# An attention and gated-convolution kernel: loads on ScalarE spaced by the transfer in front of them, and a new order of the work

## The chip, the cores and the metric

The kernel runs on one core of a Trainium2 chip. The time is that of the device in microseconds, from three runs; beside it stands one execution that the hardware profiler recorded.

## The reference, cut to what matters

```python
B, N, m, C = 4, 12800, 32, 128                 # x is B x N x C, I is m x C
def mab(q, kv):                                # attention, scale = 1 / sqrt(C)
    a = softmax(scale * q @ kv.T)              # over the last axis, less its maximum
    return a @ kv
h = mab(I, x)                                  # 32 rows for each of the 4 batches
x1 = mab(x, h)
gate = sigmoid(sum(conv_w[k] * shift(x1, 4 - k) for k in range(5)))   # along N, causal
out = (gate * (x1 @ w_val)) @ w_out
```

## The kernel before

The 12800 positions of a batch are cut into four strips of 3200, and each strip into seven or eight chunks of 128 to 480 positions; the four strips of a chunk are worked on together. Chunk c of batch b is written (b, c). Each chunk is loaded twice: transposed (`xt`, 0.70 to 0.98 MB, line 392), for the scores, and with positions on the partitions (`xk`, line 404), for the weighted sums; most chunks of batch 0 have their `xk` made on TensorE from `xt` instead (L431).

The work has items, which the list `ORDER` puts in a row: `s1` (scores of the 32 inducing rows against a chunk, L456), `gm` (their maximum), `h` (weighted sum over a chunk, L523), `u`, `w`, `W`, `po` (small steps once a batch: normalise h, fold w_val, the taps and w_out into weights), `s2` (scores of a chunk against h, L718, and a softmax over 32 on VectorE, GpSimd and ScalarE, up to the fp16 halves P1 and P2, L791 and L798), `r` (a block of gate matmuls, L812, for one chunk, with the value matmuls, L821, of the chunk before), `o` (the output projection of one strip of a chunk, L922 to L924, and its eviction from PSUM, L937 on VectorE or L939 on ScalarE), `x` and `k` (make or load an `xk`), `z` (idle matmuls on zeros, L976) and `raw` (load of the weights). An `l` item loads a chunk if it isn't loaded yet; all of them stand behind the first use of their chunk, so they do nothing.

`ORDER` fixes TensorE's order. The orders of the other engines come from a planner, `Plan.lay`, at build time: it plays all operations through with costs, gives each engine the ready one that is due first (less a bias from `URGE`), and the program is emitted in that order. Nothing of the planner runs on the chip. In it `bus` is the time at which the transfers issued so far are through, and `line` the same for stores. A load is an operation of SyncE before the first `r` item and of ScalarE after it, a store (L957) of SyncE, apart from two at the end. Engines work in their own order, so an operation that waits holds up what is behind it on that engine. The list `OUTV` says which evictions go to VectorE.

The number of buffers bounds how far an engine runs ahead: 11 for `xt`, 4 for `xk`, 6 for the evicted output (`os`), 4 PSUM banks (`a`) for scores, values and outputs. An eviction waits until the store of the tile six before it has landed; the PSUM bank that it reads stays taken so long.

Of the kernel before, what the change touches and what calls it, by code (L numbers as in the profile page):

```python
# [40 lines left out]
PAGE, PAGE_AT, PAGE_TIME = 256, 20, 1.0  # L41
LAND, LAND_OUT = 3.2, 2.0
# [9 lines left out]
class Plan:  # L52
# [15 lines left out]
    def op(self, eng, dur, fn, deps=(), early=0.0, new=(), use=(), lag=None, kind=None, behind=(), steps=0, dma=None):  # L68
# [71 lines left out]
    def lay(self, deps, succ, topo, nominal):  # L140
# [18 lines left out]
        free, bus, steps = dict.fromkeys(("PE", "DVE", "ACT", "POOL"), 0.75), 1.45, -PAGE_AT  # L159
# [10 lines left out]
        while len(seq) < n:  # L170
            best = None
            for e, lst in pools.items():
                if not lst:
                    continue
                start = max(free.get(e, 0.0), min(r for r, _ in lst))
                if e == "PE":
                    w = len(wants[lst[0][1]])
# [56 lines left out]
def tile_kernel(ctx: ExitStack, tc: tile.TileContext, xt, xk, indT_in, w64, out):  # L234
# [211 lines left out]
    def s1(b, c, bank="a"):  # L446
# [21 lines left out]
    def gmax(b, g):  # L468
# [18 lines left out]
        i = PE(16, 0.17, f1, [i, i_const], [key], [m1], "strips", 0.2)  # L487
# [51 lines left out]
    def prep(b):  # L539
# [32 lines left out]
        i = PE(8, 0.42, f3, [i, i_const], [key], [Hs[-1]], lag=0.2)  # L572
# [9 lines left out]
    def prep2(b):  # L582
# [7 lines left out]
        i4 = PE(4, 0.28, f4, [ix["hT", b], iw], [key], [("hT", b)], lag=0.15)  # L590
# [46 lines left out]
    def prep3(b, e):  # L637
# [8 lines left out]
        i6 = PE(48, 0.35, f6, ix[w2][e], [key], [w2], lag=0.25)  # L646
# [13 lines left out]
    def prep_out(b):  # L660
# [13 lines left out]
        i = PE(16, 0.24, f1, [i, i_mask], [key], [dq], "strips", 0.2)  # L674
# [151 lines left out]
    def rblock(k, *starts):  # L826
# [11 lines left out]
        for lo, hi in zip(cuts, cuts[1:]):  # L838
# [20 lines left out]
            i = PE(2 * len(todo), max(spent), f, list(dict.fromkeys(deps)), new, use, "rows", 0.34)  # L859
# [43 lines left out]
    def outp(k, r):  # L903
# [9 lines left out]
        if last:  # L913
# [3 lines left out]
            i = PE(4, 1.06 / 512 * n, f, [ix["gv", b, c, r], ix["wo", b]], [key], [tg, ("wof", b)])  # L917
        else:
# [7 lines left out]
            i = PE(6, COST["out"] * n, f, [ix[g2], ix["wo", b]], [key], [g1, g2, ("wo", b)])  # L926
# [4 lines left out]
        def ev():  # L931
            if new:
# [34 lines left out]
    PE(2 * WARM, 0.43 * WARM, warm_up, [i_zero], [("a", "warm")])  # L967

    def idle(k, n):
# [8 lines left out]
        PE(2 * n, 0.216 * n, f, [], [key])  # L978
# [202 lines left out]
```

## Time and profile before

| | |
|---|---|
| median of 3 runs | 289.60 us (289.21 to 289.81) |
| the profiled execution | 289.35 us, of which the span from the first to the last instruction is 287.6 us |
| granted clock of TensorE, mean over the span | 0.988 |
| TensorE busy | 273.8 us (95%) |
| VectorE busy | 231.4 us (80%) |
| GpSimd busy | 207.9 us (72%) |
| ScalarE busy | 197.7 us (69%) |
| moved by DMA | 75.41 MB (48.56 read, 26.21 written by the instructions' account) |

Matmuls are pipelined, and the profile models their ends, so "busy" on TensorE says that it has matmuls under way. The granted clock is 1.00 at 2.4 GHz and 0.50 at 1.2 GHz. Time of an engine that is not on the chain which ended last costs nothing by itself.

### The profile page before, as it was taken

Reading aid. Unit: us, or ns where it says so; the run is one execution under the profiler, and the core shown is the slowest. Engines: PE = TensorE matmul, PEld = TensorE weight load, DVE = VectorE, ACT = ScalarE, POOL = GpSimd, SP = SyncE. Lnnn points to the kernel's source line nnn. Section 1 sums busy time; section 2 is a strip of 40 time slices with the busy share of each in tenths; the row PEclk is TensorE's granted clock in tenths of the full one; section 3 lists DMA queues with packets and bytes.
Section 4 is the critical chain, followed back from the end, with each engine's and each line's share of the span. In section 5 each row is a group of like instructions: output and inputs, shape, how many; then the busy total and the mean of one; then the engine's idle time right before and its main releaser. Section 6 shows DMA issues by size and latency. Waiting matters only on the chain.

```text
span 287.6 us, 10037 instructions
## 1 busy us (share of the span) xinstructions
PE 273.8 (95%) x4123; PEld 143.0 (50%) x4123; DVE 231.4 (80%) x541; ACT 197.7 (69%) x299; POOL 207.9 (72%) x236
## 2 busy tenths in 40 slices
PE   8989798999998999999699999999999999999998
PEld 2658345555544555575234645474444444444543
DVE  1558789989888999879389999879878999876861
ACT  2547159577657887877519886996876987777662
POOL 2000467998686799976736998988898999989650
PEclk9999889999999999999979999999999999999999
DMA  7999998988997788899955988604252224434437
GB/s 289 424 416 417 413 421 318 345 316 276 397 370 265 220 285 315 266 388 411 389 202 167 336 305 294 249 9 171 96 200 92 98 98 171 168 134 174 173 137 273
DMA packets 24493, 75.41 MB, mean 262 GB/s; under 512 B 2816, under 2 KB 17664, under 8 KB 24448
## 3 DMA queue, kind: packets, MB, share of 16 engines
q1 hardware_dynamic: 19120, 42.03, 37.9%
q10 hardware_dynamic: 5328, 32.75, 31.4%
q8 instruction: 32, 0.52, 0.7%
q14 instruction: 13, 0.11, 0.1%
HBM read 48.56 MB, written 26.21 MB: 260 GB/s over the span
## 4 chain that ended last, share of the span: by engine, by line
PE 76%; DVE 10%; DMA 9%; issue 2%; ACT 1%; POOL 1%; ACTq 0%; DVEq 0%; POOLq 0%
PE g L812 22%; DMA out_dram<-os 9%; PE a L523 8%; PE a L718 7%; PE a L456 7%; PE a L922 7%; PE a L924 6%; PE a L923 6%; PE a L821 4%; PE g L431 3%; DVE tg L881 2%; PE g L976 2%; DVE os L937 1%; PE a L965 1%; DVE ss L464 1%
## 5 line engine op out<-in xcount | busy, mean ns | idle before, releaser
L899 POOL TENSOR_TENSOR gl<-tg,gh 128x960 f16<-128x960 f32 (+4 forms) x56 | 104.7, 1882 | 14.0 <-PE a L924 7.8
L812 PE MATMUL g<-P,W 32*128 32x480 f16 (+4 forms) x1740 | 103.4, 345 | 1.0 <-POOL P L798 0.7
L881 DVE SCALAR_TENSOR_TENSOR tg<-tg,a 128x480 f32<-128x480 f32 (+4 forms) x116 | 65.5, 601 | 10.1 <-PE a L821 8.9
L812 PEld LDWEIGHTS <-W 32*128 32x128 f16 x1740 | 51.4, 92 | 42.7 <-issue 12.3
L894 ACT CAST gh<-tg 128x960 f16<-128x960 f32 (+4 forms) x56 | 51.9, 929 | 20.3 <-DVE tg L881 19.5
L871 ACT ACTIVATE tg<-g,gsc 128x960 f32<-128x960 f32 (+4 forms) x58 | 55.9, 993 | 3.5 <-PE g L812 3.2
L937 DVE TENSOR_SCALAR os<-a,osc 128x480 f32<-128x480 f32 (+4 forms) x61 | 39.3, 672 | 9.5 <-DMA out_dram<-os 6.6
L821 PE MATMUL a<-P,W 32*128 32x480 f16 (+4 forms) x348 | 41.8, 344 | 1.0 <-ACT os L939 0.7
L922 PE MATMUL a<-gh,wo 128*128 128x480 f16 (+4 forms) x112 | 39.6, 354 | 1.8 <-DVE os L937 1.1
L923 PE MATMUL a<-gh,wo 128*128 128x480 f16 (+4 forms) x112 | 39.3, 351 | 0.0
L924 PE MATMUL a<-gl,wo 128*128 128x480 f16 (+4 forms) x112 | 39.2, 351 | 0.0
L939 ACT ACTIVATE os<-a,osc 128x480 f32<-128x480 f32 (+4 forms) x47 | 28.4, 622 | 10.8 <-DMA out_dram<-os 5.3
L798 POOL TENSOR_TENSOR P<-pt,P 128x480 f16<-128x480 f32 (+4 forms) x29 | 29.9, 1035 | 4.9 <-ACT P L791 4.4
L456 PE MATMUL a<-xt,indT 128*32 128x480 f32 (+4 forms) x232 | 30.0, 589 | 3.4 <-DVE os L937 2.2
L780 POOL TENSOR_TENSOR e<-e,z 128x480 f32<-128x480 f32 (+4 forms) x29 | 27.2, 939 | 4.0 <-DVE z L773 1.6
L735 POOL TENSOR_TENSOR e<-e,m 128x480 f32<-128x480 f32 (+4 forms) x29 | 27.1, 938 | 3.8 <-DVE m L729 3.5
L718 PE MATMUL a<-xt,hT 128*32 128x480 f32 (+4 forms) x232 | 28.9, 563 | 0.7 <-ACT os L939 0.6
L523 PE MATMUL a<-xk,et 128*32 128x129 f32 x800 | 28.3, 275 | 1.2 <-issue 1.0
L523 PEld LDWEIGHTS a<-xk,et 128*32 128x32 f32 x800 | 24.2, 109 | 7.9 <-issue 3.2
L741 ACT ACTIVATE e<-e 128x480 f32<-128x480 f32 (+4 forms) x29 | 16.7, 575 | 13.1 <-POOL e L735 10.9
L464 DVE TENSOR_SCALAR_CACHE_REDUCE ss<-a 128x480 f32<-128x480 f32 (+4 forms) x29 | 17.4, 606 | 9.0 <-PE a L456 8.8
L922 PEld LDWEIGHTS <-wo 128*128 128x128 f16 x112 | 11.3, 101 | 21.7 <-issue 12.7
(111 smaller groups left out, 325.3 us busy)
## 6 DMA issues: line engine op xcount, KB each, us to landing
out_dram<-os SPq DMA_DIRECT2D x52, 240.0 KB, 2.5
xt<-in_xt_dram ACTq DMA_DIRECT2D x11, 960.0 KB, 7.8
out_dram<-os SPq DMA_DIRECT2D x44, 224.0 KB, 2.7
xk<-in_xk_dram ACTq DMA_DIRECT2D x9, 967.5 KB, 7.6
xk<-in_xk_dram ACTq DMA_DIRECT2D x7, 903.0 KB, 7.3
xt<-in_xt_dram SPq DMA_DIRECT2D x6, 960.0 KB, 11.5
xt<-in_xt_dram ACTq DMA_DIRECT2D x5, 896.0 KB, 7.1
xk<-in_xk_dram SPq DMA_DIRECT2D x4, 903.0 KB, 12.5
```

What stands on the lines that cost most here:

```text
L456: T.matmul(s[32 * r:32 * r + 32, :n], c_["indT"], x[:, o:o + n // 32, r, :], start=True, stop=True)
L523: T.matmul(t[32 * s:32 * s + 32, :P + 1], e[:, 32 * i:32 * i + 32], x[:, m + i, :], start=i < R, stop=i >= nb - R)
L718: T.matmul(s[32 * r:32 * r + 32, :n], st["hT", b], x[:, m:m + nb, r, :], start=True, stop=True)
L812: T.matmul(st[f"g{r // 2}", b, c][:, r % 2, :n], st["W", b][q, w, k, :], st[("P1", "P2")[e]][q, o:o + n], start=u == 0, stop=u == len(taps ...
L821: T.matmul(st["a", "v", b, c, r][:, :n], st["W", b][q, w, TAPS, :], st[("P1", "P2")[e]][q, o:o + n], start=u == 0, stop=u == 2)
L871: S.activation(t[:, :, :n], st[f"g{p}", b, c][:, :, :n], AF.Tanh, scale=st["gsc", b])
L881: V.scalar_tensor_tensor(t, t, 1.0, st["a", "v", b, c, r][:, :n], ALU.add, ALU.mult)
L894: S.copy(sb(pw, g1, [P, 2, CW], F16)[:, :, :n], st[tg][:, :, :n])
L899: G.tensor_tensor(sb(pw, g2, [P, 2, CW], F16)[:, :, :n], st[tg][:, :, :n], st[g1][:, :, :n], ALU.subtract)
L922: T.matmul(t, w[:, 0], st[g1][:, q, :n], start=True, stop=False)
L923: T.matmul(t, w[:, 1], st[g1][:, q, :n], start=False, stop=False)
L924: T.matmul(t, w[:, 0], st[g2][:, q, :n], start=False, stop=True)
```

## The change

In the planner, a load on ScalarE is ready only when the transfers in front of it take at most `DEPTH` = 2.4 us. Its picture of DMA is another: how long after its transfer a load or a store counts as landed, how long a store waits behind loads, and no more charge for instruction pages (with it the `steps` argument of every TensorE operation goes). `ORDER`, the starts of the value matmuls within the `r` blocks, `URGE` and `OUTV` are new. The 289 items of `ORDER` are the same but for those starts. `OUTV` has 71 evictions on VectorE in place of 65. In `outp` the tile of the last chunk's outputs is allocated by whichever of its two evictions comes first.

```diff
-PAGE, PAGE_AT, PAGE_TIME = 256, 20, 1.0
-LAND, LAND_OUT = 3.2, 2.0
+LAND, LAND_OUT, DEPTH = 4.0, 1.8, 2.4
...
-        free, bus, steps = dict.fromkeys(("PE", "DVE", "ACT", "POOL"), 0.75), 1.45, -PAGE_AT
+        free, bus = dict.fromkeys(("PE", "DVE", "ACT", "POOL"), 0.75), 1.45
...
+                if e == "ACT":
+                    lst[:] = [(max(r, bus - DEPTH) if ops[i]["dma"] and ops[i]["dma"][1] == "load" else r, i) for r, i in lst]
                 start = max(free.get(e, 0.0), min(r for r, _ in lst))
...
-            if e == "PE":
-                steps += ops[i]["steps"]
-                while steps >= PAGE:
-                    steps -= PAGE
-                    bus = max(bus, start) + PAGE_TIME
             if ops[i]["dma"]:
-                xfer, kind = ops[i]["dma"]
+                xfer, what = ops[i]["dma"]
                 free[e] = start + ISSUE[e]
-                if kind == "load":
+                if what == "load":
                     bus = max(bus, start) + xfer
-                    end[i] = max(bus, start + 0.5) + (1.7 if start < 10.0 else LAND)
+                    end[i] = max(bus, start + 0.5) + (LAND if start > 10.0 else 1.7 if bus < 14.2 else 2.8)
                 else:
-                    both = bus > start
-                    line = max(line, start) + xfer * (1 + both)
-                    bus += xfer * both
+                    begin = max(line, start)
+                    line = begin + xfer + min(max(bus - begin, 0.0), 4.6 if line <= start else 2.3)
+                    bus = max(bus, begin) + xfer
                     end[i] = line + LAND_OUT
...
         def ev():
-            if new:
+            if os not in st:
...
 ORDER = [
-    ('z', 5, 2), ('s1', 0, 0), ('s1', 0, 2), ('x', 0, 2), ('s1', 0, 1), ('x', 0, 0), ('gm', 0, 0), ('s1', 0, 3),
-    ('x', 0, 1), ('h', 0, 2), ('s1', 0, 4), ('x', 0, 3), ('s1', 0, 7), ('h', 0, 0), ('h', 0, 1), ('gm', 0, 1),
-    ('s1', 0, 6), ('s1', 0, 5), ('k', 0, 4), ('raw',), ('gm', 0, 3), ('k', 0, 5), ('x', 0, 6), ('h', 0, 4),
-    ('gm', 0, 2), ('h', 0, 3), ('x', 0, 7), ('h', 0, 6), ('h', 0, 5), ('h', 0, 7), ('s1', 1, 0), ('z', 4, 1),
-    ('u', 0), ('z', 0, 1), ('w', 0), ('s2', 0, 0), ('s2', 0, 1), ('s1', 1, 2), ('l', 1, 0), ('s2', 0, 2), ('po', 0),
-    ('W', 0, 0), ('W', 0, 1), ('s1', 1, 1), ('s1', 1, 3), ('r', 0), ('s2', 0, 3), ('gm', 1, 0), ('r', 1, 1, 9),
...
+    ('z', 5, 2), ('s1', 0, 0), ('z', 0, 1), ('s1', 0, 1), ('s1', 0, 2), ('x', 0, 2), ('s1', 0, 4), ('x', 0, 0),
+    ('gm', 0, 0), ('s1', 0, 7), ('x', 0, 1), ('s1', 0, 3), ('gm', 0, 3), ('x', 0, 3), ('h', 0, 0), ('h', 0, 1),
+    ('gm', 0, 1), ('s1', 0, 6), ('h', 0, 2), ('s1', 0, 5), ('raw',), ('k', 0, 4), ('k', 0, 5), ('x', 0, 6),
+    ('gm', 0, 2), ('h', 0, 3), ('h', 0, 4), ('x', 0, 7), ('h', 0, 6), ('h', 0, 5), ('h', 0, 7), ('s1', 1, 0),
+    ('u', 0), ('z', 4, 1), ('w', 0), ('s2', 0, 0), ('s2', 0, 1), ('s1', 1, 2), ('s2', 0, 2), ('s1', 1, 1),
+    ('W', 0, 0), ('l', 0, 1), ('W', 0, 1), ('s1', 1, 3), ('r', 0), ('l', 1, 0), ('po', 0), ('s2', 0, 3),
...
```

## Rows read from the trace of the kernel before

**Rows 1.** Busy time of each engine in stretches of the span. The columns: the stretch and its length, then busy microseconds and instructions of TensorE's matmuls (PE), its weight loads (PEld), VectorE (DVE), ScalarE (ACT) and GpSimd (POOL), TensorE's granted clock, DMA's busy share and its GB/s.

```profile
0.00:30.00 30.00, 26.36 (x370) 16.48 (x373) 15.09 (x49) 14.59 (x23) 3.56 (x25) 1.00 0.96 387
30.00:50.00 20.00, 17.10 (x322) 8.63 (x316) 17.41 (x59) 11.32 (x25) 12.50 (x25) 0.91 0.95 386
50.00:88.00 38.00, 37.15 (x622) 19.51 (x614) 33.84 (x86) 25.29 (x40) 31.99 (x39) 1.00 0.94 342
90.00:139.00 49.00, 49.00 (x830) 28.24 (x823) 43.44 (x95) 38.48 (x59) 40.34 (x41) 1.00 0.87 312
149.00:270.00 121.00, 120.90 (x1811) 59.18 (x1807) 106.16 (x223) 96.84 (x137) 106.40 (x100) 1.00 0.46 168
270.00:287.60 17.60, 15.27 (x132) 8.07 (x124) 9.18 (x16) 7.27 (x11) 6.65 (x4) 1.00 0.58 213
```

**Rows 2.** The chain of work that ended last, three of its pieces: start, length, what.

```profile
79.01 9.38 DMA out_dram<-os
...
111.92 2.36 PE a L456 x24
...
133.57 9.75 DMA out_dram<-os
```

**Rows 3.** The timeline from 132 to 152 us: start, busy time, engine, line, operation, tiles, shapes and count; in brackets the engine's idle time before it and what ended it.

```profile
140.52 0.68 DVE L937 TENSOR_SCALAR os<-a,osc 128x448 f32<-128x448 f32 x1 [2.36 <-DMA out_dram<-os]
141.26 0.35 PE L922 MATMUL a<-gh,wo 128*128 128x448 f16 x1 [1.05 <-DVE os L937]
...
143.45 0.68 DVE L937 TENSOR_SCALAR os<-a,osc 128x448 f32<-128x448 f32 x1 [2.24 <-DMA out_dram<-os]
...
144.19 3.15 PE L456 MATMUL a<-xt,indT 128*32 128x480 f32 x16 [2.20 <-DVE os L937]
...
145.45 0.64 ACT L939 ACTIVATE os<-a,osc 128x448 f32<-128x448 f32 x1 [4.45 <-DMA out_dram<-os]
```

**Rows 4.** Busy time of each engine in three stretches, columns as in rows 1.

```profile
140.00:142.00 2.00, 0.93 (x5) 0.19 (x2) 0.68 (x1) 1.00 (x2) 2.00 (x2) 1.00 1.03 384
142.00:144.20 2.20, 0.01 (x3) 0.02 (x3) 0.75 (x2) 0.00 (x0) 0.08 (x1) 0.85 0.99 367
144.20:149.00 4.80, 4.80 (x40) 1.36 (x44) 3.86 (x13) 0.96 (x2) 1.38 (x4) 0.72 0.71 270
```

**Rows 5.** The timeline from 77 to 92 us, columns as in rows 3.

```profile
88.47 0.66 ACT L939 ACTIVATE os<-a,osc 128x480 f32<-128x480 f32 x1 [0.90 <-DMA out_dram<-os]
...
89.19 0.38 PE L821 MATMUL a<-P,W 32*128 32x480 f16 x2 [0.73 <-ACT os L939]
```

**Rows 6.** Line 957, the store of an output tile, in three stretches (issued from 78 to 83, from 130 to 150 and from 190 to 280 us): its DMAs, and the time from issue to landing.

```profile
L957 SPq DMA_DIRECT2D out_dram<-os x6: 332/363/442, 78.6 to 82.1; - x6
...
DMA to landing us min/median/max: 7.0/9.3/9.7
...
L957 SPq DMA_DIRECT2D out_dram<-os x10: 332/332/339, 133.1 to 146.7; - x10
...
DMA to landing us min/median/max: 2.5/6.9/11.2
...
L957 SPq DMA_DIRECT2D out_dram<-os x50: 332/332/1307, 193.5 to 277.4; - x50
...
DMA to landing us min/median/max: 1.9/2.1/4.3
```

**Rows 7.** The timeline of ScalarE from 124 to 130 us; ACTq is its queue, which issues the loads. The first and the last of the rows with loads; those left out are two more loads of xk.

```profile
124.19 0.33 ACTq L404 DMA_DIRECT2D xk<-in_xk_dram  x1
124.42 0.93 ACT L894 CAST gh<-tg 128x896 f16<-128x896 f32 x1
125.25 1.00 ACT L871 ACTIVATE tg<-g,gsc 128x896 f32<-128x896 f32 x1
...
127.77 1.63 ACTq L392 DMA_DIRECT2D xt<-in_xt_dram  x3
129.44 0.53 ACTq L404 DMA_DIRECT2D xk<-in_xk_dram  x1
```

**Rows 8.** DMA from 133 to 140 us (packets, amount, mean rate), and the loads issued from 124 to 150 us: tile, queue, count, size of one, time to landing (median).

```profile
DMA packets 569, 2.81 MB, mean 402 GB/s; under 512 B 58, under 2 KB 216, under 8 KB 567
...
xk<-in_xk_dram ACTq DMA_DIRECT2D x2, 967.5 KB, 6.8
xt<-in_xt_dram ACTq DMA_DIRECT2D x2, 960.0 KB, 10.9
...
xk<-in_xk_dram ACTq DMA_DIRECT2D x1, 903.0 KB, 6.0
xk<-in_xk_dram ACTq DMA_DIRECT2D x1, 709.5 KB, 16.0
xt<-in_xt_dram ACTq DMA_DIRECT2D x1, 704.0 KB, 13.6
```

**Rows 9.** The evictions of outputs, two groups of the page: line, engine, operation, tiles, shapes, count | busy, mean ns of one | idle time before them.

```profile
L937 DVE TENSOR_SCALAR os<-a,osc 128x480 f32<-128x480 f32 (+4 forms) x61 | 39.3, 672 | 9.5 <-DMA out_dram<-os 6.6
...
L939 ACT ACTIVATE os<-a,osc 128x480 f32<-128x480 f32 (+4 forms) x47 | 28.4, 622 | 10.8 <-DMA out_dram<-os 5.3
```

**Rows 10.** Line 404, the load of an xk, issued from 115 to 116.5 us: its DMAs, and the time to landing; and from TensorE's timeline from 120 to 126 us the matmuls that use xk (L523).

```profile
L404 ACTq DMA_DIRECT2D xk<-in_xk_dram x2: 334/361/388, 115.3 to 115.7; - x2
...
DMA to landing us min/median/max: 4.8/6.3/7.9
...
122.50 0.97 PE L523 MATMUL a<-xk,et 128*32 128x129 f32 x27
...
123.98 2.25 PE L523 MATMUL a<-xk,et 128*32 128x129 f32 x66
```

More of the change, by code (lines that the diff above doesn't have):

```diff
@@ L66, in urge, with op @@
         return self.urges[code]
-    def op(self, eng, dur, fn, deps=(), early=0.0, new=(), use=(), lag=None, kind=None, behind=(), steps=0, dma=None):
+    def op(self, eng, dur, fn, deps=(), early=0.0, new=(), use=(), lag=None, kind=None, behind=(), dma=None):
         i = len(self.ops)
@@ L249, in tile_kernel, with PE @@
     st = {}
-    def PE(steps, dur, fn, deps=(), new=(), use=(), kind="full", lag=None):
-        i = plan.op("PE", dur, fn, deps, 0.0, new, use, lag, kind, steps=steps)
+    def PE(dur, fn, deps=(), new=(), use=(), kind="full", lag=None):
+        i = plan.op("PE", dur, fn, deps, 0.0, new, use, lag, kind)
         pe.append(i)
@@ L485, in f1 @@
                 T.matmul(t[32 * r:32 * r + 32, :R * n], c_["pick"], st[m1][:, :, :n], start=True, stop=True)
[L487 removed]
+        i = PE(0.17, f1, [i, i_const], [key], [m1], "strips", 0.2)
         def f2():
@@ L570, in f3 @@
             T.matmul(t[:, M:2 * M], H[:, P:].broadcast_to([P, P]), c_["pick"], start=True, stop=True)
-        i = PE(8, 0.42, f3, [i, i_const], [key], [Hs[-1]], lag=0.2)
+        i = PE(0.42, f3, [i, i_const], [key], [Hs[-1]], lag=0.2)
         def f4():
@@ L588, in f4 @@
             T.matmul(pt(key)[:, :M], c_["wval"], st["hT", b], start=True, stop=True)
-        i4 = PE(4, 0.28, f4, [ix["hT", b], iw], [key], [("hT", b)], lag=0.15)
+        i4 = PE(0.28, f4, [ix["hT", b], iw], [key], [("hT", b)], lag=0.15)
         def g0():
@@ L644, in f6 @@
                     T.transpose(t[32 * r:32 * r + 32, q, :], st[w2][:, e, q, :], c_["ident"])
-        i6 = PE(48, 0.35, f6, ix[w2][e], [key], [w2], lag=0.25)
+        i6 = PE(0.35, f6, ix[w2][e], [key], [w2], lag=0.25)
         def f7():
@@ L672, in f1 @@
                 T.matmul(t[32 * r:32 * r + 32, :P], c_["ones"], st[dq], start=True, stop=True)
-        i = PE(16, 0.24, f1, [i, i_mask], [key], [dq], "strips", 0.2)
+        i = PE(0.24, f1, [i, i_mask], [key], [dq], "strips", 0.2)
         def f2():
@@ L857, in f @@
                     fn(*a)
-            i = PE(2 * len(todo), max(spent), f, list(dict.fromkeys(deps)), new, use, "rows", 0.34)
+            i = PE(max(spent), f, list(dict.fromkeys(deps)), new, use, "rows", 0.34)
             for fn, b, c, r, u in todo:
@@ L924, in f @@
                 T.matmul(t, w[:, 0], st[g2][:, q, :n], start=False, stop=True)
-            i = PE(6, COST["out"] * n, f, [ix[g2], ix["wo", b]], [key], [g1, g2, ("wo", b)])
+            i = PE(COST["out"] * n, f, [ix[g2], ix["wo", b]], [key], [g1, g2, ("wo", b)])
         v = 4 * k + r in OUTV
@@ L976, in f @@
                 T.matmul(t, c_["zero"][:, :P], c_["zero"], start=True, stop=True)
-        PE(2 * n, 0.216 * n, f, [], [key])
+        PE(0.216 * n, f, [], [key])
     def S1(b, c, bank="a"):
@@ L1057 @@
 URGE = {
-    "tile_kernel.f_ind": 58.5,
-    "tile_kernel.f_zero": 84,
-    "tile_kernel.f_const": 146,
-    "tile_kernel.f_mask": 16,
-    "tile_kernel.warm_up": -59,
-    "load_xt.f": -129,
-    "tile_kernel.f_wload": 40.5,
-    "weights.start": 101.5,
-    "weights.<lambda>": 87.5,
-    "weights.cmax": 203,
-    "idle.f": 242.5,
-    "s1.f": -357.5,
-    "s1.g": -84.5,
-    "make_xk.ones": 240,
-    "make_xk.tp": 138,
-    "make_xk.ev": 106.5,
-    "make_xk.<lambda>": 32.5,
-    "gmax.f0": 500.5,
@@ L1121 @@
-    "outp.f": -11.5,
-    "outp.ev": -377.5,
-    "outp.store": -185.5,
+    "tile_kernel.f_ind": 74,
+    "tile_kernel.f_zero": 71.5,
+    "tile_kernel.f_const": 141,
+    "tile_kernel.f_mask": 4.5,
+    "tile_kernel.warm_up": -39,
+    "idle.f": 277.5,
+    "load_xt.f": -159.5,
+    "s1.f": -368,
+    "s1.g": -88.5,
+    "make_xk.ones": 234,
+    "make_xk.tp": 165.5,
+    "make_xk.ev": 114.5,
+    "make_xk.<lambda>": -19,
+    "gmax.f0": 503.5,
+    "gmax.f1": -83,
+    "gmax.f2": 52.5,
+    "e1.f": 9,
@@ new lines @@
+    "e1.tr": 198,
+    "h.f": -136,
+    "h.acc": 309,
+    "tile_kernel.f_wload": 19.5,
+    "weights.start": 82,
+    "weights.<lambda>": 119,
+    "weights.cmax": 244,
+    "load_xk.f": -269,
+    "prep.f0": 177.5,
+    "prep.<lambda>": -249.5,
+    "prep.f1": -124.5,
+    "prep.f2": 22.5,
+    "prep.f3": -117.5,
+    "prep.f4": 173.5,
+    "prep2.f4": 42.5,
+    "prep2.g0": 82.5,
+    "prep2.g1": -196,
+    "prep2.<lambda>": -83,
+    "prep2.g2": 75.5,
+    "prep2.g3": -26,
+    "prep2.f8": -89.5,
@@ new lines @@
+    "s2.f": -216.5,
+    "s2.tin": 193.5,
+    "s2.mx": 65.5,
+    "s2.sub": -65,
+    "s2.ex": 76.5,
+    "s2.sm": -31.5,
+    "s2.sa": -60,
+    "s2.rz": 86.5,
+    "s2.nm": -0.5,
+    "s2.tout": 42.5,
+    "s2.hi": -258.5,
+    "s2.lo": -99,
+    "prep_out.f0": -67,
+    "prep_out.f1": -21,
+    "prep_out.f2": -81.5,
+    "prep_out.f3": 137.5,
+    "prep_out.<lambda>": -256.5,
+    "prep_out.f4": -149.5,
+    "prep3.f6": -248,
+    "prep3.f7": -69.5,
+    "rblock.f": -503.5,
+    "rblock.th": -114,
@@ L1124 @@
+    "rblock.gv": -230,
+    "halves.hi": -8.5,
+    "halves.lo": 208,
+    "outp.f": -0.5,
+    "outp.ev": -376.5,
+    "outp.store": -197.5,
 }
```

59 lines of the change are left out of this document (7 added, 52 removed), and 70 rows, old and new, of tables (ORDER, OUTV).

## The prediction

> **What bounds the kernel now.** I read the busy time by stretch first. TensorE is the bound: it is busy for all of 90 to 139 us and for 120.90 of 121 us from 149 to 270, while VectorE, the next, stands at 43.44 of 49 and 106.16 of 121 [rows 1]. So only what makes TensorE stop, or run at its lower clock, sets the end. That leaves four stretches: 0 to 30 (3.64 us idle), 30 to 50 (2.90 us idle and a granted clock of 0.91), 50 to 88 (0.85 us idle), and the gaps that the first table leaves out, around 89 and from 139 to 149 us.
>
> The second view is the chain of work that ended last. Twice it runs through a store of an output tile instead of an engine: 9.38 us from 79.01 and 9.75 us from 133.57 [rows 2]. The reader is to see that a 240 KB store takes longer there than anything an engine does.
>
> The third is the timeline around the ends of those stores. At 140.52 VectorE starts an eviction after 2.36 us of waiting for a store, and TensorE, which needs the PSUM bank, goes on at 141.26 after 1.05 us idle. At 143.45 the same again: 2.24 us on VectorE, 2.20 us on TensorE before 144.19. ScalarE waits 4.45 us for a third store [rows 3]. In 142 to 144.2 us TensorE is busy for 0.01 us; after it the granted clock is 0.72 over 4.8 us [rows 4]. The earlier place is smaller: ScalarE waits 0.90 us for a store and TensorE 0.73 us for ScalarE, up to 89.19 [rows 5].
>
> The fourth is landing times. From 193 us on, when no loads run, a store lands 2.1 us after its issue (median; 1.9 at best). From 133 to 147 us it is 6.9 (worst 11.2), from 78 to 83 us 9.3 [rows 6]. What is in front is seven loads that ScalarE issues between 124.19 and 129.44 [rows 7]. They hold 2 x 967.5 + 903 + 709.5 + 2 x 960 + 704 = 6171.5 KB, or 6.32 MB, which at the 402 GB/s of that stretch is 15.7 us of transfer [rows 8]; 5.25 us of it can pass while they are issued, so some 10.5 us stand in front of the next store. The store of 133.57 should then land near 140 + 2; it landed at 143.3. Stores and loads share one line here, in the order of issue or nearly.
>
> The Trainium skill ("DMA: Bandwidth & Descriptors", section "Queues, rings and completion order") says otherwise: each DMA engine takes packets in turn from the queue rows that have work, so a store on SyncE's row should get its turns whatever ScalarE's row holds. By that rule a store would land within a few microseconds behind any pile of loads, and the change would have nothing to save; the landings of 9 to 11 us above speak against it, and the measurement decides. It stands below as a rival.
>
> **The change, part by part.**
>
> *Loads spaced.* In the plan a load on ScalarE may now start only when at most 2.4 us of transfer are in front of it. One load is 967.5 KB, or 0.99 MB, at 402 GB/s 2.46 us [rows 8]. So at most 2.4 + 2.46 = 4.9 us stand in front of a store that follows, and it lands at most 4.9 + 2.1 = 7.0 us after its issue, on average about half the pile later than alone (4.5 us), instead of up to 11.2. The number of loads, their bytes and the cost of issuing them on ScalarE (0.33 us in the cheapest row of [rows 7]) stay; they only stand elsewhere in its order.
>
> *What that is worth at 139 to 149 us.* TensorE's two waits are 1.05 + 2.20 = 3.25 us [rows 3]. The clock behind them: 0.72 is a mix of full and half speed (2.4 and 1.2 GHz), so 0.56 of 4.8 us, 2.7 us, ran at half, and half of that, 1.35 us, is lost [rows 4]. As a second count, sixteen score matmuls took 3.15 us there [rows 3] where 24 take 2.36 at full clock [rows 2], so 16 take 1.57: 1.58 us. I take 1.4. Does any of it stay? The first wait ended with the landing of the store issued at 133.08, and VectorE had begun to wait at 140.52 - 2.36 = 138.16, so a store of up to 5.1 us would not have been felt; at 7.0 it would be felt for 1.9 us on VectorE. TensorE had 2.36 - 1.05 = 1.3 us of cover, so it would lose at most 0.6. The second: VectorE idle from 143.45 - 2.24 = 141.21, store issued at 133.57, so 7.6 us were free, more than 7.0. Residue 0 to 0.6; I take 0.2, since the average store is well under 5.1.
>
> *At 88 us.* ScalarE idle from 88.47 - 0.90 = 87.57, its store issued at 79.01: 8.6 us free, over 7.0. All of TensorE's 0.73 us [rows 5] goes.
>
> *The new order of the work.* The same 289 items stand in the new list and the same idle fillers, so TensorE's matmuls stay as they are. Counted in the two lists, the changes between kinds of TensorE work go from 109 to 107 and the cuts of the gate blocks from 160 to 156; no row prices one, and the nearest are gaps of tenths of a microsecond, so this is 0 to -0.5, taken as -0.1. What I cannot work out is which small waits the new order has. The old one lost 0.85 us in 50 to 88, nothing in 90 to 139, 0.10 in 149 to 270 [rows 1]. Bounds are 0 and, with 0.85 lost in each of the two long stretches that lose almost nothing now, 1.7; I take +0.6, nearer to the rows.
>
> *The first 50 us.* The transposed loads on SyncE come in another order (the 320-column chunk second), the weights' load moves ahead of one key-value load, a filler matmul moves to the front, and a score block of batch 1 moves ahead of the weight transposes. DMA is busy for 0.96 and 0.95 of the time there [rows 1], and the bytes are the same, so the last chunk of batch 0 lands when it did. Lost there today: 3.64 + 2.90 us idle and 0.18 of 20 us at half clock, 1.8 us. One score block is 2.36 / 3 = 0.8 us [rows 2]: the order can fill or open about one such hole. From -1.0 to +1.0, taken as 0.
>
> *Evictions moved.* Six more of the 116 output evictions go to VectorE, each 672 ns instead of 622 on ScalarE [rows 9]: 4.0 us more on VectorE and 3.7 less on ScalarE, spread over the span. The cover is TensorE's own work; VectorE is at 89% in both 50 to 88 (33.84 of 38) and 90 to 139 [rows 1]. I take 0; if the cover is gone, a few evictions at 0.67 us each show, 2 us together. The rest of the diff (the old model of instruction pages, the steps argument, who allocates the last chunk's tile) issues nothing.
>
> *Sum.* 3.25 + 1.4 + 0.73 = 5.4 us go. Against the profiled execution's 289.35: 289.35 - 5.4 + 0.2 - 0.1 + 0.6 = 284.7. The median is 0.25 us above that execution, so **285.0 us**.
>
> **Rivals.**
>
> *A load comes late (slower).* Spacing works by holding loads back. Most have room, but two key-value loads of batch 2, issued at 115.3 and 115.7, land 4.8 and 7.9 us later, at 120.1 and 123.6 [rows 10]; by the order of the list their matmuls begin at 122.50 and about 124.9, the latter inside the 66 that start at 123.98. Room: 2.4 and 1.3 us. ScalarE works in order, so a load that waits for its slot also waits for the tanh and the cast ahead of it (1.00 and 0.93 us, [rows 7]). Held back by the whole 4.9 us and by those two, it lands 6.8 us later: TensorE waits 6.8 - 1.3 = 5.5 us and loses 1.4 on the clock, 285.0 + 6.9 = 291.9. It decides from a loss of 5.2 us (290.2). For it: the small room. Against it: the same chunks can be issued earlier in another order, since what precedes them in transfer is then shorter.
>
> *The stall comes back smaller.* Up to 7.0 us is still more than the 5.1 us that six output buffers gave at 133. If four runs of evictions meet it, TensorE loses 4 x 0.6 = 2.4 us and once the clock, 1.4: 288.8 less the 0.2 already counted, 288.6.
>
> *VectorE takes over.* With the stalls gone its 89% becomes more, and it has 4.0 us more work: +2 us, 287.0.
>
> *The pile was not the cause.* If landing does not depend on what is in front, nothing of the 5.4 us goes: 289.6 with 0.5 for the order, 290.1. The rule of the Trainium skill that is told above ("DMA: Bandwidth & Descriptors", "Queues, rings and completion order") would lead here. Against it stand the landings of [rows 6]: 9.3 and 6.9 us with loads in front, 2.1 without.
>
> **How the numbers follow.** The forecast has 0.57, from 283.4 (early part 1.0 better, waits of the order 0.6 less) to 286.6. The smaller stall has 0.14, VectorE 0.09, the late load 0.14, no effect 0.06. 0.2% is 0.6 us, about what a measurement of this kernel tells from no change. Forecast, smaller stall and VectorE hold 0.80, so the range goes from 283.0 to 289.0. Faster: 0.57 + 0.09 + most of 0.14, and a little of the late load when it is short: 0.78. Same: 0.07, from the no-effect case and a late load that cancels the gain. Slower: 0.15.
>
> **What would show it.** Right: no burst of loads on ScalarE closer than about 2 us; stores from 60 to 180 us landing within 7 us of issue; no wait of VectorE or ScalarE for an output store over 1 us; granted clock 1.00 from 50 us to the end; the chain of waits without a store of 9 us. Wrong: TensorE idle before the L523 matmuls of batches 2 or 3 with a key-value load as the cause, new waits of TensorE on VectorE in 50 to 139 us, or a lower clock before 50 us than 0.91.

## The result, and the profile after

Four runs of the changed kernel have a median of 281.36 us (280.13 to 282.61), four of the kernel before beside them 289.71. The ratio is 0.9702, with a 95% interval of 0.9636 to 0.9768: 8.35 us faster, where 4.6 were forecast, and 1.6 us below the range on record. The profiled execution took 282.61 us, span 280.8, mean granted clock 0.994 (before: 289.35, 287.6, 0.988).

TensorE by stretch, which answers to [rows 1] and [rows 4]. The columns are the stretch, its length, and the busy time and count of TensorE, its weight loads, VectorE, ScalarE and GpSimd, then the granted clock, the DMA share and the rate:

```profile
0.00:30.00 30.00, 26.99 (x385) 16.78 (x385) 16.80 (x55) 14.98 (x25) 3.72 (x26) 1.00 0.95 385
30.00:50.00 20.00, 16.48 (x340) 9.53 (x339) 16.93 (x56) 10.89 (x24) 12.95 (x26) 0.91 1.01 392
50.00:88.00 38.00, 37.41 (x619) 18.79 (x615) 34.67 (x86) 28.24 (x44) 31.38 (x35) 1.00 0.95 348
88.00:90.00 2.00, 2.00 (x41) 0.89 (x34) 2.00 (x5) 0.12 (x2) 2.00 (x2) 1.00 0.83 312
90.00:139.00 49.00, 48.91 (x799) 27.05 (x801) 44.04 (x102) 38.36 (x58) 42.07 (x45) 1.00 0.90 334
139.00:149.00 10.00, 9.48 (x127) 4.66 (x120) 8.80 (x23) 5.82 (x8) 6.54 (x9) 1.00 0.56 191
149.00:262.00 113.00, 113.00 (x1697) 55.21 (x1696) 100.79 (x209) 87.77 (x125) 100.59 (x94) 1.00 0.48 176
```

The holes at 88 and at 139 to 149 us are closed: 0.52 us idle is left of the second, and the clock stays at its upper level behind it. The first 50 us lose about what they lost (6.53 us idle against 6.54, granted clock 0.91 in 30 to 50 both times).

The evictions, two groups of the page, and the waits of evictions for output stores in the whole span (sum, times, longest). They answer to [rows 9], where 6.6 and 5.3 us stand:

```profile
L933 DVE TENSOR_SCALAR os<-a,osc 128x480 f32<-128x480 f32 (+4 forms) x67 | 42.9, 663 | 6.4 <-PE a L920 5.0
...
L935 ACT ACTIVATE os<-a,osc 128x480 f32<-128x480 f32 (+4 forms) x41 | 25.1, 628 | 7.8 <-PE a L920 5.8
```

```profile
DVE os L933 <- DMA out_dram<-os: 1.1, 1, 1.1
```

The waits for stores fell from 11.9 to 1.1 us. The stores themselves did not come home earlier. All stores issued one by one from 60 to 180 us, before:

```profile
L957 SPq DMA_DIRECT2D out_dram<-os x50: 332/333/1285, 60.4 to 178.2; - x50
...
DMA to landing us min/median/max: 2.4/6.4/11.2
```

and after:

```profile
L953 SPq DMA_DIRECT2D out_dram<-os x54: 332/332/817, 60.0 to 178.9; - x54
...
DMA to landing us min/median/max: 1.9/5.9/11.4
```

Median 6.4 against 5.9, worst 11.2 against 11.4. In the chain of work that ended last (start, length, what) one such store still stands, and behind it the one short wait that is left, on ScalarE's and TensorE's timeline:

```profile
130.62 9.66 DMA out_dram<-os
```

```profile
140.36 0.63 ACT L935 ACTIVATE os<-a,osc 128x448 f32<-128x448 f32 x1 [1.82 <-PE a L452]
```

```profile
140.17 0.36 PE L808 MATMUL g<-P,W 32*128 32x448 f16 x2
141.05 0.36 PE L817 MATMUL a<-P,W 32*128 32x448 f16 x2 [0.51 <-ACT os L935]
```

The store of 130.62 lands at 140.28, the eviction starts at 140.36 (its row names TensorE for the wait, the chain names the store), and TensorE idles 0.51 us. The loads on ScalarE's queue still go out in groups:

```profile
122.33 1.60 ACTq L388 DMA_DIRECT2D xt<-in_xt_dram  x2
124.03 0.39 ACTq L400 DMA_DIRECT2D xk<-in_xk_dram  x1
127.53 0.33 ACTq L400 DMA_DIRECT2D xk<-in_xk_dram  x1
```

**Runs at one clock.** The mean granted clock of a run comes in steps, and the time goes with it. In the profiled executions a step is one stretch in which the clock falls to its lower level: two in the kernel before (from about 34 and 143 us, 0.988), one in the changed kernel (from about 33 us, 0.994), none in its second profile below (1.000). Of the 64 runs of the kernel before that stand beside the experiments, those at 1.000 have a mean of 287.4 us (4 runs), at 0.994 288.7 (19), at 0.988 289.8 (28), at 0.982 291.2 (12), and one at 0.977 took 294.0. Runs at one clock still differ, at 0.994 from 286.8 to 290.5 us. The changed kernel, both sets of runs together, has 280.3 at 1.000 (7 runs) and 282.2 at 0.994 (3). So the change is worth about 7.1 us at full clock and 6.4 at 0.994; the rest of the 8.35 is that the median run of before stands at 0.988 and that of after between 0.994 and 1.000.

### The profile page after: what moved, and what is told of

It reads as the page before. It is cut to its first block, busy times and chain, and to the rows that moved or that the text cites. A ratio compares the mean times of both kernels' runs of the same rounds, so it can differ in the third digit from the quotient of the medians.

```text
span 280.8 us, 10049 instructions
## 1 busy us (share of the span) xinstructions
PE 270.8 (96%) x4123; PEld 141.4 (50%) x4123; DVE 233.9 (83%) x547; ACT 195.1 (69%) x293; POOL 207.2 (74%) x236
## 4 chain that ended last, share of the span: by engine, by line
PE 85%; DMA 6%; DVE 4%; POOL 3%; issue 1%; ACT 1%; SPq 0%; POOLq 0%; ACTq 0%
PE g L808 27%; PE a L519 8%; PE a L918 8%; PE a L714 8%; PE a L920 7%; PE a L919 7%; PE a L452 7%; PE a L817 5%; DMA out_dram<-os 3%; PE g L427 3%; DMA xt<-in_xt_dram 2%; PE g L972 1%; PE a L911 1%; PE a L640 1%; POOL gl L895 1%
## 5 line engine op out<-in xcount | busy, mean ns | idle before, releaser
L808 PEld LDWEIGHTS <-W 32*128 32x128 f16 x1740 | 50.7, 92 | 42.7 <-issue 11.0
L933 DVE TENSOR_SCALAR os<-a,osc 128x480 f32<-128x480 f32 (+4 forms) x67 | 42.9, 663 | 6.4 <-PE a L920 5.0
L935 ACT ACTIVATE os<-a,osc 128x480 f32<-128x480 f32 (+4 forms) x41 | 25.1, 628 | 7.8 <-PE a L920 5.8
L452 PE MATMUL a<-xt,indT 128*32 128x480 f32 (+4 forms) x232 | 27.8, 554 | 1.8 <-DMA xt<-in_xt_dram 1.1
L519 PE MATMUL a<-xk,et 128*32 128x129 f32 x800 | 28.3, 275 | 0.7 <-issue 0.6
L714 PE MATMUL a<-xt,hT 128*32 128x480 f32 (+4 forms) x232 | 27.9, 562 | 0.0
L519 PEld LDWEIGHTS a<-xk,et 128*32 128x32 f32 x800 | 24.3, 109 | 7.0 <-issue 2.5
L918 PEld LDWEIGHTS <-wo 128*128 128x128 f16 x112 | 11.2, 100 | 21.0 <-issue 12.9
```

Of the source, the lines that this page charges most:

```text
L452: T.matmul(s[32 * r:32 * r + 32, :n], c_["indT"], x[:, o:o + n // 32, r, :], start=True, stop=True)
L519: T.matmul(t[32 * s:32 * s + 32, :P + 1], e[:, 32 * i:32 * i + 32], x[:, m + i, :], start=i < R, stop=i >= nb - R)
L714: T.matmul(s[32 * r:32 * r + 32, :n], st["hT", b], x[:, m:m + nb, r, :], start=True, stop=True)
L808: T.matmul(st[f"g{r // 2}", b, c][:, r % 2, :n], st["W", b][q, w, k, :], st[("P1", "P2")[e]][q, o:o + n], start=u == 0, stop=u == len(taps ...
L918: T.matmul(t, w[:, 0], st[g1][:, q, :n], start=True, stop=False)
```

## The experiments

### Which part of the change does it

Five kernels take the change apart. The first is the changed kernel without the bound on transfer in front of a load:

```
-LAND, LAND_OUT, DEPTH = 4.0, 1.8, 2.4
+LAND, LAND_OUT, DEPTH = 4.0, 1.8, 1000.0
```

> The changed kernel with the spacing of loads undone alone: its lists and its picture of DMA stay, but a load may start whatever is in front of it. Theory A (the spacing is what removed the stalls): loads pile up again, stores land after 9 to 16 us, TensorE waits 3 to 6 us for evictions, 285 to 289 us. Theory B (the new lists removed them, because they were chosen with stores that take long): 281 to 283 us, stores as slow as in the changed kernel or slower, without TensorE waiting.

Measured: 285.12 us against 290.05, ratio 0.9835 (0.9788 to 0.9881); 284.55 at clock 1.000.

The second is the kernel before with the bound alone, its own lists and costs:

```
-LAND, LAND_OUT = 3.2, 2.0
+LAND, LAND_OUT, DEPTH = 3.2, 2.0, 2.4
...
+                if e == "ACT":
+                    lst[:] = [(max(r, bus - DEPTH) if ops[i]["dma"] and ops[i]["dma"][1] == "load" else r, i) for r, i in lst]
```

> The kernel before with the spacing of loads alone, at 2.4 us in its own old picture of DMA. Theory A: the pile of seven loads at 124 to 129 us is gone and with it most of the two stalls, 284 to 286 us. Theory B: the old lists still run into stores that land late, 287 to 291 us.

Measured: 289.51 us, ratio 1.0011 (0.9970 to 1.0053). From 130 to 150 us no store lands later than 8.0 us after its issue, but the median is 7.4 (before 6.9); the wait at 140 us shrinks, and others open behind it. Its stretches, and TensorE's timeline at one of the new waits:

```profile
139.00:149.00 10.00, 8.41 (x115) 3.54 (x114) 7.10 (x20) 3.31 (x5) 5.12 (x8) 1.00 0.97 357
149.00:270.00 121.00, 118.77 (x1733) 57.38 (x1732) 104.23 (x217) 95.70 (x136) 104.95 (x98) 1.00 0.46 167
```

```profile
156.90 0.34 PE L823 MATMUL a<-P,W 32*128 32x448 f16 x1 [0.96 <-ACT os L941]
```

Before, 149 to 270 us lost 0.10 us [rows 1]; here it is 2.23.

The third is the changed planner with the lists of before (the order, the urges, and which evictions VectorE takes); the fourth, the other way round, the planner of before with the lists of after (and the test that allocates the last chunk's tile). The first line that the third changes, against the changed kernel:

```
-    ('z', 5, 2), ('s1', 0, 0), ('z', 0, 1), ('s1', 0, 1), ('s1', 0, 2), ('x', 0, 2), ('s1', 0, 4), ('x', 0, 0),
+    ('z', 5, 2), ('s1', 0, 0), ('s1', 0, 2), ('x', 0, 2), ('s1', 0, 1), ('x', 0, 0), ('gm', 0, 0), ('s1', 0, 3),
...
```

> The changed kernel's planner (spacing and new picture of DMA) with the lists of the kernel before (order, biases, evictions). Theory A: 284 to 286 us. Theory B: 287 to 291 us, with a stall behind a store somewhere between 60 and 150 us.

Measured: 294.26 us, ratio 1.0141 (1.0090 to 1.0193). TensorE is busy for 34.48 of 40 us from 50 to 90, with one wait of 3.09 us on GpSimd at 62.15. No eviction waits for a store.

> The kernel before with the new lists alone (order, biases, evictions, and who allocates the last chunk's tile); planner without spacing and with its old picture of DMA. If the lists work by themselves: 283 to 286 us. If they work only with the planner that they were chosen for: 287 to 291 us, with waits of TensorE between 35 and 75 us.

Measured: 285.23 us against 289.38, ratio 0.9822 (0.9772 to 0.9872), as without the bound: the rest of the planner's new costs moves nothing by itself.

The last of this group is the changed kernel with only the older choice of evictions for VectorE (65 of the 116 instead of 71):

```
-    2, 3, 5, 6, 7, 8, 11, 12, 13, 14, 15, 21, 23, 26, 27, 29, 30, 31, 32, 33, 34, 36, 37, 38, 42, 43, 48, 51, 53,
+    2, 5, 6, 8, 9, 10, 11, 13, 14, 22, 23, 24, 25, 30, 31, 32, 33, 34, 37, 38, 39, 42, 43, 45, 48, 49, 52, 54, 56,
...
```

> The changed kernel with the kernel before's choice of which evictions go to VectorE (65 of 116 in place of 71). If the choice is worth as little as on record (0 to 2 us): 280 to 282.5 us. If the lists hold together only as they were chosen with each other and the planner: 283 us or more, with new waits of TensorE.

Measured: 293.48 us against 289.55, ratio 1.0175 (1.0131 to 1.0219), all six runs at clock 0.994. TensorE's longest new wait:

```profile
65.83 0.61 PE L714 MATMUL a<-xt,hT 128*32 128x480 f32 x4 [2.38 <-ACT os L935]
```

The eviction that it waits for did not wait for a store; no eviction does in this run.

What follows from the five: the lists without the bound give 2.4 to 2.9 us at full clock (287.4 to 284.95, the mean of three runs of the fourth kernel, or to 284.55, one run of the first), the bound with these lists another 4.3 to 4.7 (to 280.3; at 0.994, 285.7 to 282.2, it is 3.5), the bound without them nothing, and with all the lists taken back, or the choice of evictions alone, the kernel is slower than before. No part has a price of its own.

The waits of evictions for stores tell more than the times. They sum to 11.9 us before and 1.1 after (none in its second profile below), and in the five kernels, in the order above, to 2.7, 3.0, 0, 3.1 and 0 us. All five have lost most of them, and the two slowest kernels have none: what these lose stands in other waits. Only all parts together remove the waits for stores without opening others. Nor is the bound's gain mostly one of stores. Without it (first kernel) TensorE idles 13.4 us, and 9.5 in a second profile of the changed kernel at the same clock. Of these 4.0 us, 1.7 lie before 50 us, 1.5 from 50 to 90 and 0.8 from 90 to 150, and the longest wait without the bound is for VectorE's product of gates and values (tile `tg`):

```profile
47.38 1.84 PE L519 MATMUL a<-xk,et 128*32 128x129 f32 x54 [1.98 <-DVE tg L877]
```

### Whether it is where the loads stand

The planner lays everything else anew when a load is held back, so two more kernels move loads only. One takes the finished program of after and moves each load on ScalarE up to where its buffer is free (below); the other takes the program of before and moves loads down, in the same manner, until at most 2.4 us of loads are in front:

```
+    for i in [i for i in seq if ops[i]["eng"] == "ACT" and ops[i]["dma"] and ops[i]["dma"][1] == "load"]:
...
+        to = next((p for p in range(low, k) if ops[seq[p]]["eng"] == "ACT" and plan.at[seq[p]] >= ready), k)
+        seq.insert(to, seq.pop(k))
```

> The changed kernel's program; only the loads on ScalarE are moved up in ScalarE's order to where their buffers are free in the plan, so that they pile up; the order of everything else on every engine stays. If the late loads by themselves save time (stores land earlier): 283 to 286 us, with new waits of TensorE for evictions, and stores that land after up to 15 us. If spacing helped only because the planner then laid the other operations elsewhere: 280 to 282 us like the changed kernel.

Measured: 282.56 us against 288.96, ratio 0.9776 (0.9738 to 0.9815). The changed kernel, run again beside it:

> The changed kernel once more, beside the others on one chip: 280.3 us in runs at a mean granted clock of 1.00, 282.4 at 0.994, median between.

Measured: 280.59 us, ratio 0.9713 (0.9672 to 0.9754). At clock 1.000 the two have means of 281.9 and 280.3 us: the place of the loads alone is worth 1.6 us (1.0 at 0.994, 283.2 against 282.2). The profiled executions do not settle where. With loads early TensorE idles 0.73 us from 50 to 90 and 0.37 from 90 to 139,

```profile
50.00:90.00 40.00, 39.27 (x643) 19.46 (x639) 36.51 (x89) 28.08 (x43) 33.39 (x36) 1.00 0.92 346
90.00:139.00 49.00, 48.63 (x791) 27.08 (x793) 43.44 (x102) 37.50 (x58) 41.10 (x44) 1.00 0.93 338
```

and in the changed kernel's second profile 0 and 0.11:

```profile
50.00:90.00 40.00, 40.00 (x642) 19.58 (x644) 37.50 (x90) 29.89 (x45) 33.84 (x35) 1.00 0.92 340
90.00:139.00 49.00, 48.89 (x820) 27.18 (x815) 44.04 (x105) 36.68 (x57) 42.73 (x47) 1.00 0.95 355
```

But in its first profile it idles 0.59 and 0.09 us there, and another 0.52 from 139 to 149, as much in all as with loads early.

The other kernel, the program of before with its loads moved down:

> The kernel before; only its loads on ScalarE are moved down in ScalarE's order so that at most 2.4 us of loads are in front of each by the planner's own times; everything else stays where it was. By the sum on record: the two stalls shrink to under 1 us, 284 to 286 us. If stores still take 7 us or more, and stall elsewhere: 287 to 290 us.

Measured: 288.88 us, ratio 0.9976 (0.9942 to 1.0010). The stores from 128 to 140 us still take a median of 9.1 us, and TensorE stops twice as before:

```profile
139.35 0.35 PE L922 MATMUL a<-gh,wo 128*128 128x448 f16 x1 [1.34 <-DVE os L937]
141.61 3.43 PE L456 MATMUL a<-xt,indT 128*32 128x480 f32 x16 [1.53 <-DVE os L937]
```

The spacing goes by the planner's times; in the trace up to 2.4 MB of loads were still to move when a store was issued between 60 and 180 us, against 3.5 MB before, and evictions still wait 7.8 us for stores. So spacing the loads in the program of before does not make its stores land early, and does not save its stall.

### What the late stores cost

In both kernels the stores of all chunks but the last are cut to 32 of 128 partitions (the rest of the output is left out):

```
-                nc.sync.dma_start(out[b, :, r, FIRST[b][c]:FIRST[b][c] + n], st[os][:, :n])
+                nc.sync.dma_start(out[b, :32, r, FIRST[b][c]:FIRST[b][c] + n], st[os][:32, :n])
```

> The kernel before, storing 32 of the 128 partitions of each output tile but for the last chunk (a quarter of the packets and bytes; the rest of the output is left out), so that stores hardly share the DMA engines; the order on each engine is unchanged. If late stores cost what the trace says (3.3 + 0.7 us idle and one fall of the clock of 1.4): 284 to 286 us and no wait of TensorE for an eviction at 88 or 140 us. If the gain of the change came from elsewhere: above 288 us.

Measured: 281.57 us against 289.38, ratio 0.9698 (0.9644 to 0.9751); mean at clock 1.000 281.2. No eviction waits for a store, and TensorE does not stop:

```profile
50.00:90.00 40.00, 40.00 (x672) 20.97 (x664) 36.45 (x91) 29.28 (x47) 33.50 (x37) 1.00 0.78 290
90.00:135.00 45.00, 45.00 (x746) 25.80 (x739) 39.61 (x89) 34.87 (x54) 39.05 (x39) 1.00 0.74 272
135.00:150.00 15.00, 14.90 (x192) 6.96 (x195) 14.22 (x38) 10.52 (x17) 10.81 (x14) 1.00 0.60 212
```

> The changed kernel with the same quarter of the stores (the rest of the output is left out). If the change has removed nearly all that late stores cost, 279.5 to 281.5 us, under 1 us better than the changed kernel at the same granted clock; if it has removed only part, 277 to 279 us.

Measured: 279.12 us, ratio 0.9626 (0.9568 to 0.9683); mean at clock 1.000 278.9. At full clock the stores' traffic costs the kernel before 287.4 - 281.2 = 6.2 us and the changed one 280.3 - 278.9 = 1.4. That is 4.8 of the 7.1 us. The other 2.3 (281.2 to 278.9) are what the rest of the change gives, with the order, the evictions and the loads all placed anew, without any late store. At 0.994 the picture is the same, with single runs of the cut kernels: 288.7 - 282.6 = 6.1 us and 282.2 - 281.1 = 1.1 us. Cut stores also leave the loads more of the DMA, so 6.2 is the price of all that the stores' traffic does, not of the two waits alone.

### How stores and loads share the DMA

Packets by queue in the kernel before, q10 the loads from ScalarE, q1 the stores from SyncE (packets, MB, share of the engines). First 133 to 136 us, with the issues of that stretch:

```profile
q10 hardware_dynamic: 182, 1.22, 101.9%
...
out_dram<-os SPq DMA_DIRECT2D x3, 224.0 KB, 10.8
```

then 136 to 140 us:

```profile
q10 hardware_dynamic: 211, 1.29, 79.3%
q1 hardware_dynamic: 174, 0.27, 18.2%
```

For some 3 us after the first store's issue at 133.08 no packet of a store moves. Then stores move beside the loads, in like numbers of packets; but a load's packet holds 6.1 KB and a store's 1.6, so the stores get 0.27 of 1.56 MB. In the changed kernel the counts are equal too in some stretches, 201 and 201 from 82 to 86 us. Over others they are not, as in its 136 to 140 us, where for part of the time the stores move almost alone:

```profile
q10 hardware_dynamic: 192, 1.09, 66.6%
q1 hardware_dynamic: 339, 0.50, 32.9%
```

The silence at the start does not grow with the pile. In the kernel before six stores were issued from 60 to 180 us while loads were still to move and no other store was under way. Their first packet came 3.2 to 4.2 us after the issue: 3.6 us with 3.5 MB of loads in front (133.08 us) and 3.7 with 1.0 MB (153.68). Without loads it came after 0.8 us. For the store of 153.68, the packets from 153.6 to 157.3 us:

```profile
q10 hardware_dynamic: 117, 0.90, 89.4%
```

If the share of the bytes is what makes stores late, smaller packets of loads must help. In two kernels the loads of batches 2 and 3 are cut into runs of 2 to 3.6 KB (a gap of 16 elements between runs in DRAM); the first left one chunk, of 352 positions, whole:

```
+                early.dma_start(to.rearrange("p (g l) -> p g l", g=g),
+                                xt[b, :, at_:at_ + g * (l + GAP)].rearrange("p (g l) -> p g l", g=g)[:, :, :l])
```

> The kernel before; for batches 2 and 3 the loads of chunks of 480 and 448 positions read runs of about 2.5 and 3.6 KB a partition in place of 7.2 to 7.7 KB (pieces with a gap between them in DRAM); a store's run is 1.9 KB. If loads and stores go through in the order of issue, a store behind the seven loads takes as long as before (7 to 11 us) and the time stays at 289 to 290 us. If the DMA engines take one packet from each queue in turn, a store beside loads gets two to three times the bytes that it got, the stores of 133 to 147 us land after 4 to 7 us, the stall of TensorE at 140 us shrinks from 3.3 us idle to under 1 us, and the time is 284 to 287 us.

Measured: 288.52 us against 290.05, ratio 0.9914 (0.9876 to 0.9953). The stall at 140 us stayed; the chunk left whole is one of the loads in front of it.

> The kernel before; all loads of batches 2 and 3 but those of first chunks' xt read pieces of 2 to 3.6 KB a partition (the shorter experiment left the last two loads of the pile at 5.6 KB). By the earlier look, queues that both have packets send equal numbers of them, after some 3 us in which a new store sends none. Then a store's share of the bytes beside loads goes from about a fifth to over a third, the stores of 133 to 147 us land 2 to 3 us earlier than the 7 to 11 us of before, TensorE's idle time at 140 us falls from 3.3 us to 1 to 2, and the time is 1.5 to 3 us below the kernel before. If stores go behind all loads issued before them, nothing moves: within 0.5 us of before.

Measured: 287.89 us against 289.55, ratio 0.9962 (0.9928 to 0.9996). Packets from 137 to 142 us, and the stores issued from 128 to 140:

```profile
q10 hardware_dynamic: 563, 1.13, 59.3%
q1 hardware_dynamic: 561, 0.83, 44.3%
```

```profile
L971 SPq DMA_DIRECT2D out_dram<-os x6: 332/332/404, 132.9 to 138.8; - x6
...
DMA to landing us min/median/max: 6.3/7.8/9.0
```

Equal numbers of packets again, and now 42% of the bytes for the stores. The worst landing falls from 11.2 [rows 6] to 9.0 us, and the two waits at 140 us (1.05 and 2.20 us idle [rows 3]) become 1.31 us idle in 139 to 149:

```profile
90.00:139.00 49.00, 46.99 (x774) 26.37 (x763) 41.07 (x91) 36.38 (x56) 40.21 (x40) 1.00 0.88 312
139.00:149.00 10.00, 8.69 (x114) 3.35 (x114) 7.83 (x21) 3.89 (x6) 5.13 (x8) 1.00 0.72 270
```

The first row gives it back: 2.01 us idle before 139, where there was none (1.73 of it at 132.22, for VectorE's product of gates and values and not for a store). That packets take turns by number while both queues move them is shown in both kernels, and so is that the stores' share of the bytes then goes by the size of a packet; the silence of 3 us is not explained by it.

> The changed kernel with the same smaller pieces. What late stores still cost it was 1.4 us at equal clock, so 279.3 to 280.4 us; if pieces of 2 KB slow the loads themselves, 280.5 to 282.

Measured: 280.55 us, ratio 0.9720 (0.9679 to 0.9760): no different from the changed kernel (0.9713 and 0.9702).

### The fall of the clock at 33 us

TensorE idles around 30 us and the clock falls at 33 to 37 us in some runs. Two kernels put more idle matmuls there, ten in one and five (three and two) in the other. The second has no `z` in front of `s1` 0, 5. The lines of the first:

```
-    ('gm', 0, 1), ('s1', 0, 6), ('h', 0, 2), ('s1', 0, 5), ('raw',), ('k', 0, 4), ('k', 0, 5), ('x', 0, 6),
+    ('gm', 0, 1), ('s1', 0, 6), ('h', 0, 2), ('z', 7, 3), ('s1', 0, 5), ('raw',), ('k', 0, 4), ('k', 0, 5), ('x', 0, 6),
...
-    ('u', 0), ('z', 4, 1), ('w', 0), ('s2', 0, 0), ('s2', 0, 1), ('s1', 1, 2), ('s2', 0, 2), ('s1', 1, 1),
+    ('z', 6, 4), ('u', 0), ('z', 4, 4), ('w', 0), ('s2', 0, 0), ('s2', 0, 1), ('s1', 1, 2), ('s2', 0, 2), ('s1', 1, 1),
```

> The changed kernel with ten more idle matmuls where TensorE waits between 19 and 33 us (3 ahead of the last scores of batch 0, 4 ahead of the normalising step, 3 more behind it). If the lower clock of 33 to 37 us, which some runs have (282.4 us) and others not (280.3 us), follows from TensorE's idle time just before: all runs at a mean clock of 1.00 and 279.8 to 281 us. If not: the same two levels, or 0.3 to 1 us more where the fillers stand in the way.

Measured: 280.73 us against 289.38, ratio 0.9677 (0.9618 to 0.9736); four runs of four at clock 1.000.

> The changed kernel with five more idle matmuls, 3 ahead of the normalising step of batch 0 and 2 more behind it. If the fall of the clock at 33 us follows from the waits at 29 to 32 us: every run at 1.00, and 280.0 to 280.6 us, 0.2 to 0.5 below ten fillers and some 0.8 below the changed kernel's median. If not, some runs at 0.994 and 282 us.

Measured: 280.98 us against 288.96, ratio 0.9727 (0.9685 to 0.9768); five of six at 1.000, as with none in the set run beside it (280.59, five of six). Whether the idle time there makes the clock fall is not settled: too few runs fall. Neither is faster than the change.

## Why the prediction was right and wrong

**Right.** TensorE as the bound; the two places, 88 and 140 us, and that what stands there goes; the clock at 1.00 from 50 us on; the first 50 us at 0 (6.54 us idle before, 6.53 after). The late load did not come: no wait of TensorE before the L519 matmuls names an xk (the longest from 50 us on, 0.59 us at 51.12, names nothing). VectorE did not take over, at 44.04 of 49 us. Among the signs named, the groups of loads, the landings beyond 7 us, the store of 9.66 us in the chain and the wait of 1.12 us on VectorE came out against the forecast, although the time was better.

**The step that failed: "at most 4.9 us stand in front of a store that follows, and it lands ... 7.0 us after its issue".** Its first half came out nearly: when a store was issued between 60 and 180 us, at most 1.9 MB of loads were still to move, 4.8 us at 402 GB/s (2.1 MB with a load whose issue had just begun), against 3.5 MB before. Its second half did not. Landings are 1.9/5.9/11.4 us after and were 2.4/6.4/11.2; the store of 77.15 landed after 11.0 us with 1.1 MB of loads and two stores in front. The step rested on "stores and loads share one line here, in the order of issue or nearly". The counts of packets say otherwise: 174 of stores beside 211 of loads while the pile of loads was still in the queue, and a first packet that came no sooner behind 1.0 MB of loads (3.7 us) than behind 3.5 (3.6 us). The rule that the prediction set against its own ("DMA: Bandwidth & Descriptors" of the Trainium skill, section "Queues, rings and completion order": packets taken in turn from the queue rows) is what the equal counts agree with, 561 beside 563 in the kernel with small packets; the silence before them it does not explain, and whether a packet of the profile is a packet of that section is not shown. It lost its case in the prediction because a store landed late all the same. An order of issue is not needed for that: a store first waits some 3 us, and then, taking turns by packet, 1.6 KB beside 6.1 KB, gets a sixth to a fifth of the bytes as long as both queues move packets (0.27 of 1.56 MB before; 0.34 of 1.66 MB from 82 to 86 us after). So spacing alone was worth nothing (289.51 and 288.88 us). The rival "the pile was not the cause" came nearer on the mechanism and was wrong on the time, since it took the stall for bound to the landings. That the stalls went all the same is, for this step, luck.

**The term with the wrong sign: the new order, "I take +0.6".** Its bounds, 0 and 1.7 us lost, left no room for a gain beyond the 0.1 beside it. The stalls went because the plan as a whole is another: with landings as late as before, evictions no longer run into them (waits for stores 11.9 us before, 1.1 after). Parts of it remove these waits too, but lose the time elsewhere: lists without the bound 285.1, bound without lists 289.5, lists of before under the new planner 294.3, old evictions 293.5. Without late stores the rest of the change is worth 2.3 us more in the means at full clock, and 1.2 in the two profiled executions (280.48 and 279.32). Of the 1.2, 0.8 is idle time in the first 50 us (6.82 and 6.00), which differs by 0.6 between two executions of the changed kernel (6.53 and 7.11); so what this gain is made of stays open.

**The term that was too small: late stores.** The sum had 3.25 + 0.73 us of TensorE's idle time, less 0.2, and 1.4 of clock. By the cut stores, 6.2 us hung on the stores before and 1.4 still do: 4.8 at full clock, with no clock term in it. At full clock the sum was 3.25 + 0.73 - 0.2 + 0.1 - 0.6 = 3.3 us and the kernels differ by 7.1. Of the gap 1.0 is this term (4.8 where 3.8 stood), and 2.8 the order (2.3 gained where 0.5 was lost). Part of the difference may be how an idle row is read. The ends of matmuls are modelled: the wait at 140.17 above is 0.51 us in its row, while the matmuls before and behind it start 0.88 us apart. In the profiled pair the execution is 6.74 us shorter; idle time is 3.8 less (13.8 to 10.0 us of span less busy time), the clock 1.8 (0.012 of 287.6 against 0.006 of 280.8), and 1.2 stand in no row.

**The clock.** The forecast took one fall of 1.4 us away and kept the one at 30 to 50 us. The profiled pair did just that (0.91 in 30 to 50 both times). The median did not: half the first four runs of the changed kernel stand at 1.000, without any fall. Of the 3.6 us between 285.0 and 281.36, 2.1 are between 284.7 and the 282.61 of the profiled execution, 1.25 between that and the median of its runs, and 0.25 were added for the median of before.

**Still open.** Why a store's first packet comes 3 to 4 us after its issue when loads run, and what lets the clock fall at 33 us in some runs and not in others. The bound gives 2.7 us and more beside the place of the loads (4.3 less 1.6): the profiles show in which stretches TensorE's idle time shrinks, but not why the planner's other choices under the bound do that.

## What to carry to other kernels

When a store lands late beside loads, look when its first packet moves and count packets by queue before you speak of a pile. Here the first packet came as late behind 1 MB of loads as behind 3.5, and while counts were equal the bytes went by the size of a packet; fewer loads in front did not help. Sum the waits that the change is aimed at in every experiment, beside the time: a kernel that has lost them all can still be slower. A part of a planned schedule has no price of its own, so take parts back both ways (old lists with the new plan, new lists with the old) before you add up terms. To price a whole class of waits, shrink the transfer that causes it in both kernels; the rows of idle time understated it here.

## What the runs showed of the hardware

While both queues moved packets they shared the DMA in nearly equal numbers (loads and stores 211 and 174, 201 and 201, 563 and 561), whatever a packet held; over stretches in which the loads moved few they did not (192 and 339). A store issued while loads were still to move sent its first packet 3.2 to 4.2 us later, as late with 1.0 MB in front as with 3.5; without loads it did so after 0.8 us and landed after 2.1 (median) [rows 6]. The means of one kernel's runs go from 287.4 to 294.0 us in steps of the mean granted clock, each step 1.1 to 2.8 us.
